# Output rows summed in PSUM, a scaled choice matrix, fewer products per block, and a new order, in a one-core kernel of a long convolution and a token-choice MLP

## The chip, the core and the metric

One core of a Trainium2 chip runs the program. Its engines are TensorE (PE; PEld is its weight load), VectorE (DVE), ScalarE (ACT), GpSimd (POOL) and SyncE (SP), which issues most of the transfers. The metric is the device time of one execution in microseconds; lower is better.

## The reference, cut to what matters

```python
x = A_q                                        # 2048 tokens of 640 features, bf16
sa, ca, ga, sb, cb, gb = silu(c) @ w_mod       # six rows of 640
h = layernorm(x) * (1 + ca) + sa
x = x + ga * (h * conv(h's k, v))              # shift conv of 4 taps, times v, long conv over 2048 tokens
h = layernorm(x) * (1 + cb) + sb               # second normalisation
r = h @ w_r;  idx = 8 tokens with the largest r
y = (silu(h[idx] @ w_gate) * (h[idx] @ w_up)) @ w_down * sigmoid(r[idx])
out = x + gb * (h + scatter(idx, y))
```

The last line is, for each token, `x*(1) + layernorm(x)*gb*(1+cb) + gb*sb`, and for eight tokens a further row of 640 is added in place in DRAM.

## The kernel before, in words

The features are split in five blocks of 128 (b = 0 to 4) and the tokens in 16 groups of 128 (m = 0 to 15). Each block goes through a convolution by two short Fourier stages: `C` (shift convolution as products with the diagonals `dg`, times `vN`), `KV` (folding), `G` and `X` (first stage into tile `A`), `BG` and `BX` (second stage into `HX`), `P` (pointwise product, `T` or `T2`), `BT` (inverse stage into `U`), `UW` (`U` written to DRAM, `Ud`), `LU` (read back transposed, `uA`), `AT` (last stage into `t`) and `AA` (added into `xq`, the residual rows). Block 4 is turned on the chip instead (`XT`, tiles `V`, `tT`, `xT`) and put back into `xq` by `RB`. `R` transposes a block of `xq` into `xT` and takes three sums over features (`pr`, added into `rsum`); `GR` takes products of `xT` with itself of which only the diagonal is used, the sum of squares (`ssq`).

Then comes the tail. `T` is one long task in steps: `n2v` and what follows make the reciprocal root `rs2` and the keys of the choice; `prT`, `vi`, `crow`, `cand`, `t8` find the eight largest keys; `oh32` is the choice matrix (one column per chosen token); `pX` gathers the rows by products with it; `px`, `xsf`, `xsT` turn and scale them; `pgu`, `gs`, `hh`, `hT`, `pyT`, `yT`, `py`, `delta` are the MLP; the last step is an indirect transfer by GpSimd that adds `delta` into the output in DRAM. Between these steps stand the output rows: `BS` and `BL` make `base` = `xq` + gb*sb, `N` makes the normalised row `xn` (ScalarE, or VectorE where the order says `*`), `F` multiplies two rows at a time by the gate (L926), adds the base (L928) and issues their transfer.

The order of all work is one table, `ORDER`: each word runs the next step of a task, a star moves its copy to VectorE, `:n` repeats it. Every engine runs its instructions in that order. A second table, `SLOTS`, says which buffer each new tile takes. PSUM has four tiles of two banks for passing results (`ps`), of which one is given up when the first small tile (`pq`, `pg`) is made.

## Time and profile before

| | us |
|---|---|
| median of 3 runs | 171.48 (170.65 to 174.46) |
| the profiled execution | 170.81 |
| its span in the profile | 169.0 |

The 1.8 us between the last two lie around the span. In the profile a busy share is the time in which an engine ran something; an engine with 90% may still not be the one that others wait for. The chain of waits follows the work that ended last back to its start.

### The profile page before, as it was taken

The page shows a single profiled execution, that of the slowest core. Times are in us where ns is not written, and L with a number is a line of the kernel's source. Part 1 is how long each engine was busy: PE and PEld are TensorE (multiplying, and loading weights), DVE is VectorE, ACT ScalarE, POOL GpSimd, SP SyncE. Part 2 cuts the span into 40 slices and gives each one's busy share as a digit, 9 for nine tenths or more (in the row PEclk, how much of TensorE's full clock was granted, in tenths as well). Part 3 has the DMA queues.
Part 4 walks back from the last instruction along what each step waited for, and adds up shares of the span by engine and source line. Part 5 has one row for each costly group of instructions (what it writes and reads, how often), then busy time and mean ns, then how long its engine had stood idle before and what let it go on. Part 6 is the DMA issues. An engine that isn't in the chain of part 4 may idle for free.

```text
span 169.0 us, 5171 instructions
## 1 busy us (share of the span) xinstructions
PE 144.2 (85%) x2210; PEld 113.9 (67%) x2210; DVE 152.5 (90%) x292; ACT 138.3 (82%) x157; POOL 41.3 (24%) x72
## 2 busy tenths in 40 slices
PE   7797988996989999999999999999699687946700
PEld 2395976885768778789987898898689563322600
DVE  7898999999999999799999999999979898998820
ACT  3629999998988998989999989989966826989900
POOL 8754079209998000420000000010000020000003
PEclk9999999999999999999999999999999955799955
DMA  6999999999999996592953629259927910385440
GB/s 136 206 275 158 228 190 267 287 365 175 283 363 225 307 264 175 179 297 62 263 188 124 215 104 273 77 152 353 272 85 213 303 69 4 83 277 216 155 159 2
DMA packets 54238, 33.93 MB, mean 201 GB/s; under 512 B 34049, under 2 KB 51910, under 8 KB 54214
## 3 DMA queue, kind: packets, MB, share of 16 engines
q1 hardware_dynamic: 54008, 33.58, 73.8%
q8 instruction: 17, 0.28, 0.7%
q0 software_dynamic: 80, 0.01, 0.1%
q14 instruction: 7, 0.06, 0.1%
q10 hardware_dynamic: 126, 0.01, 0.1%
HBM read 23.62 MB, written 6.83 MB: 180 GB/s over the span
## 4 chain that ended last, share of the span: by engine, by line
PE 53%; DVE 34%; issue 5%; ACT 4%; DMA 1%; POOLq 1%; DVEq 0%
PE ps L550 14%; PE ps L509 6%; PE ps L443 5%; DVE kv L89 4%; PE ps L599 4%; PE p L481 3%; PE ps L328 3%; DVE A L71 3%; DVE gF L465 3%; PE p L550 2%; DVE HX L71 2%; PE pg L675 2%; DVE st L854 2%; PE p L443 2%; DVE IT L928 2%
## 5 line engine op out<-in xcount | busy, mean ns | idle before, releaser
L73 ACT CAST HX<-ps 128x1024 bf16<-128x1024 f32 x30 | 29.9, 1042 | 1.2 <-PE ps L509 1.1
L73 ACT CAST A<-ps 128x1024 bf16<-128x1024 f32 x26 | 26.6, 1045 | 3.3 <-PE ps L443 3.2
L550 PE MATMUL ps<-IT,HX 128*128 128x256 bf16 x144 | 23.5, 273 | 0.0
L481 PEld LDWEIGHTS <-kT 128*128 128x128 bf16 x320 | 18.4, 98 | 2.1 <-issue 1.7
L73 ACT CAST U<-ps 128x1024 bf16<-128x1024 f32 (+1 forms) x19 | 16.8, 901 | 2.4 <-PE ps L550 2.0
L509 PE MATMUL ps<-A,FX 128*128 128x256 bf16 x128 | 18.3, 273 | 0.4 <-ACT A L73 0.2
L509 PEld LDWEIGHTS <-FX 128*128 128x128 bf16 x160 | 14.1, 97 | 4.1 <-issue 2.7
L550 PEld LDWEIGHTS <-HX 128*128 128x128 bf16 x160 | 14.8, 98 | 2.8 <-issue 1.0
L550 PE MATMUL ps<-IT,T 128*128 128x256 bf16 x80 | 15.3, 273 | 0.0
L854 DVE BATCH_NORM_STATS2 st<-xq 128x6 f32<-128x320 bf16 x32 | 13.4, 478 | 0.0
L522 DVE TENSOR_TENSOR HX<-HX 128x2048 bf16<-128x2048 bf16 x10 | 12.3, 1225 | 0.3
L383 POOL TENSOR_SCALAR dg<-ident,shk_f 128x128 bf16<-128x128 bf16 x16 | 9.9, 631 | 10.5 <-PE ps L481 9.4
L521 DVE TENSOR_TENSOR T<-HX 128x2048 bf16<-128x2048 bf16 x10 | 12.1, 1214 | 0.0
L481 PE MATMUL p<-dg,kT 128*128 128x128 bf16 x160 | 10.1, 219 | 0.8 <-DVE dg L383 0.7
L443 PEld LDWEIGHTS <-xA 128*64 128x64 bf16 x160 | 8.0, 109 | 3.7 <-issue 2.0
L550 PEld LDWEIGHTS <-T 128*128 128x128 bf16 x96 | 9.4, 98 | 1.1
L872 DVE TENSOR_TENSOR h<-h,modv 128x2048 bf16<-128x2048 bf16 x8 | 9.7, 1219 | 0.1
L481 PE MATMUL ps<-dg,kT 128*128 128x128 bf16 x160 | 9.8, 219 | 0.1
L353 POOL CAST bcol<-bint 40x1 f32<-40x1 int32 x1 | 0.2, 180 | 38.4 <-DVE bint L352 38.4
L73 ACT CAST A<-p 128x1024 bf16<-128x1024 f32 x9 | 9.4, 1041 | 0.0
L443 PE MATMUL ps<-RA,gF 128*64 128x256 bf16 x120 | 9.0, 278 | 0.0
L443 PEld LDWEIGHTS <-gF 128*64 128x64 bf16 x160 | 7.5, 109 | 2.2 <-issue 1.4
(280 smaller groups left out, 354.4 us busy)
## 6 DMA issues: line engine op xcount, KB each, us to landing
early<-in_w_mod_dram SPq DMA_DIRECT2D x6, 800.0 KB, 7.7
Ud<-U SPq DMA_DIRECT2D x8, 512.0 KB, 3.3
uA<-Ud SPq DMA_DIRECT2D x8, 512.0 KB, 5.1
gA<-in_A_ssm_k_dram SPq DMA_DIRECT2D x5, 512.0 KB, 8.4
vN<-in_A_v_dram SPq DMA_DIRECT2D x5, 512.0 KB, 6.0
xq<-in_A_q_dram SPq DMA_DIRECT2D x4, 640.0 KB, 8.0
wg<-in_B_w_gate_dram SPq DMA_DIRECT2D x5, 432.0 KB, 4.9
wu<-in_B_w_up_dram SPq DMA_DIRECT2D x5, 432.0 KB, 9.9
```

The source lines that it names most:

```text
L71: self.nc.vector.tensor_copy(out=out, in_=in_)
L73: self.nc.scalar.copy(out=out, in_=in_)
L89: V.tensor_tensor(out=out, in0=acc, in1=other, op=ALU.mult)
L383: (nc.gpsimd if evac.vector else V).tensor_scalar(out=dg[:, j, :], in0=ident[:], scalar1=shk_f[:, b, j:j + 1], scalar2=None, op0=ALU.mult)
L443: nc.tensor.matmul(ps[o, bb // 2, :, (bb % 2) * 8:(bb % 2) * 8 + 8].rearrange("p (k c) e -> p k c e", c=2), lhsT=src[:, 4 * g4 + bb, o], r ...
L481: nc.tensor.matmul(ps[:, i, :], lhsT=kT[:, n0 - j:n0 - j + P], rhs=diags[b][:, j, :], start=(j == 0), stop=(j == 3))
L509: nc.tensor.matmul(ps[:, i], lhsT=FX[:, k2, :], rhs=A[:, 2 * k2:2 * k2 + 2, u, :], start=True, stop=True)
L521: V.tensor_tensor(out=T2[:], in0=X, in1=Hi, op=ALU.mult)
L522: V.tensor_tensor(out=X, in0=X, in1=Hr, op=ALU.mult)
L550: nc.tensor.matmul(ps[:, i, :], lhsT=a, rhs=IT[:, k2, d:d + 2, :].rearrange("p a b -> p (a b)"), start=(n == 0), stop=(n == len(terms) - 1))
L854: V.bn_stats(out=st1[:, m, hf, :], in_=xq[:, m, hf * 320:hf * 320 + 320])
L872: V.tensor_tensor(out=hq, in0=hq, in1=row[:, None, 0:w].to_broadcast([P, 4, w]), op=op)
```

## The change

The tables `ORDER` and `SLOTS` are new throughout. Beside that:

- `R` makes only the transposed block. The three sums over features go into `GR`, which sums all five blocks in one PSUM tile. Its products with itself are 64 wide for groups 0 to 13 and 32 wide for groups 14 and 15: 36 per block, where there were 64. The diagonal is then taken by four VectorE steps over 960 columns, where two took 512.
- `BS`, `BL`, `F` and the tiles `xn` and `base` are gone. `XG` (VectorE) and `XL` (TensorE and ScalarE) make `xg` = `xq` times the gate. `NP` sums, in a PSUM tile per group of tokens, the row of `xq` (product with the identity) and a product of two rows (`gx`: the gate row and the gate*shift row) with two columns (mean term and one). `N` ends the row: starred, by one VectorE step `xg * rs2 + ps`; else by a product with the diagonal of `rs2` (`dgo`) and a ScalarE copy. `GX` and `NM` prepare the small operands.
- The choice matrix is multiplied by `rs2` before the gather. The steps `sel`, `sel2`, `psn`, `xa`, `xb` are gone; the mean comes from a sum that the ScalarE copy of `pX` accumulates, by one more small product.
- `T` has its index and sigmoid steps taken out (`TI`, near the end of the order). `WT` issues 12 products whose result nobody reads, three in mid-order and nine around the start of `T`.

```diff
 ORDER = """
-R2 R3 BS*:2 WG XT WD XT* GR R3 COL WG BS* R4 GR RB GR WG T BL N* N RB N WG T N:2 F T F:2 N* WD N F:2 N BL T N F BS F T
-F N:2 BS F T:2 F N:2 F BS N T N F:2 N BS F:2 T F T:2
+R2 XT WD R3 WG TC WG XT GX COL GR:3 WG:3 RB:2 WT GR XL WT T WT T XL NM XG T NP:2 T WD N*:2 NP XG NP N:2 XG NP XG NP N*
+NP N* NP:2 N* NP N N*:2 T NP N* NP XG NP:2 N* T NP N* XG NP N* N T N* TI T:3
...
+    def t_WT():
+        for k in range(4):
+            pw = ps_tile([P, 512])
+            for i in range(3):
+                nc.tensor.matmul(pw[:], lhsT=ident[:], rhs=FX[:, 0:4, :]..., start=True, stop=True)
+            yield
...
+    def small_products(ps, xT, first, last):
+        for m in range(M):
+            n = 64 if m < 14 else 32
+            c0 = 64 * m if m < 14 else 448 + 32 * m
+            for j in range(P // n):
+                t = xT[:, m * P + n * j:m * P + n * j + n]
+                nc.tensor.matmul(ps[n * j:n * j + n, c0:c0 + n], lhsT=t, rhs=t, ...)
+    def diagonals(ps, sq, out):
+        for (c0, c1, m0, m1, msk_) in ((0, 896, 0, 14, m64), (896, 960, 14, 16, m32)):
...
+            V.tensor_tensor(out=r(sq), in0=r(ps), in1=msk_[:, None, :].to_broadcast([P, n, w]), op=ALU.mult)
+            V.tensor_reduce(out=out[:, m0:m1], in_=r(sq), axis=mybir.AxisListType.X, op=ALU.add)
     def t_GR():
-        ps = other_ps([P, M, 32])
+        ps = small_ps([P, 1024])
         for b in range(NB):
+            xT = xTs[b].rearrange("p m t -> p (m t)")
             for m in range(M):
-                for j in range(4):
-                    t = slice(32 * j, 32 * j + 32)
-                    nc.tensor.matmul(ps[t, m, :], lhsT=xTs[b][:, m, t], rhs=xTs[b][:, m, t], ...)
+                nc.tensor.matmul(ps[:, 960 + 3 * m:963 + 3 * m], lhsT=xT[:, m * P:m * P + P], rhs=wcol[:, b, :], ...)
+            small_products(ps, xT, False if b else None, b == NB - 1)
             yield
-        V.tensor_tensor(out=sq, in0=ps[:], in1=m32[:, None, :].to_broadcast([P, M, 32]), op=ALU.mult)
-        V.tensor_reduce(out=ssq[:], in_=sq, axis=mybir.AxisListType.X, op=ALU.add)
+        V.tensor_copy(out=rsum[:], in_=ps[:, 960:1008].rearrange("p (m c) -> p m c", c=3))
...
+        diagonals(ps, tail()[:, 0:1920].bitcast(F32), ssq)
         yield
...
+    def t_XG():
+        w = (NB - 1) * P
+        for j in range(8):
+            V.tensor_tensor(out=xg(2 * j, 2)[:, :, 0:w], in0=xq[:, 2 * j:2 * j + 2, 0:w],
+                            in1=gbo[:, None, 0:w].to_broadcast([P, 2, w]), op=ALU.mult)
+            yield
+    def t_NM():
+        V.tensor_copy(out=spad..., in_=sn[:, 1, :])
+        pt = ps_tile([P, 4, P], BF)
+        for i in range(4):
+            nc.tensor.transpose(pt[:, i, :], spad[:, i, :], ident[:])
+        lT["n"] = tail()[:, 0:512].rearrange("p (i t) -> p i t", i=4)
+        evac(lT["n"], pt[:])
+        yield
...
+    def products(ps, a, b, first, last):
+        for i in range(2):
+            nc.tensor.matmul(ps[:, i, 0:320], lhsT=a, rhs=b[:, i, :], start=first, stop=last, ...)
+    def t_NP():
+        for m in range(M):
+            ps = outps[m] = ps_tile([P, 2, 512])
+            r = slice(32 * (m % 4), 32 * (m % 4) + 2)
+            products(ps, ident[:], half(xq[:, m, :]), True, False)
+            products(ps, lT["n"][r, m // 4, :], half(gx[r, :]), False, True)
+            yield
     def t_N():
         for m in range(M):
+            ps, row = outps[m], xg(m)[:, 0, :]
             if evac.vector:
-                V.tensor_scalar(out=xn(m), in0=xq[:, m, :], scalar1=rs2[:, m:m + 1], scalar2=nm2[:, m:m + 1], ...)
+                V.scalar_tensor_tensor(out=half(row), in0=half(row), scalar=rs2[:, m:m + 1], in1=ps[:, :, 0:320],
+                                       op0=ALU.mult, op1=ALU.add)
             else:
-                nc.scalar.activation(out=xn(m), in_=xq[:, m, :], func=ACT.Identity, scale=rs2[:, m:m + 1], ...)
+                dg = ring.tile([P, 4, P], BF, name="dgo", tag="dg", bufs=2)
+                V.tensor_scalar(out=dg[:, 0, :], in0=ident[:], scalar1=rs2[:, m:m + 1], scalar2=None, op0=ALU.mult)
+                products(ps, dg[:, 0, :], half(row), False, True)
+                nc.scalar.copy(out=half(row), in_=ps[:, :, 0:320])
+            if m % 2:
+                nc.sync.dma_start(out=out_d[:, m - 1:m + 1, :], in_=xg(m - 1, 2))
             yield
-    def t_F():
-        for j in range(8):
-            u = xn(2 * j, 2).rearrange("p (m d) -> p m d", m=2)
-            V.tensor_tensor(out=u, in0=u, in1=gbo[:, None, :].to_broadcast([P, 2, D]), op=ALU.mult)
-            yield
-            V.tensor_tensor(out=u, in0=u, in1=h_["base", j // 4][...], op=ALU.add)
-            nc.sync.dma_start(out=out_d[:, 2 * j:2 * j + 2, :], in_=u)
...
+        V.tensor_tensor(out=onehot, in0=onehot, in1=rs2[:, :, None].to_broadcast([P, M, NSEL]), op=ALU.mult)
...
-        V.tensor_tensor(out=sel, in0=onehot..., in1=sn..., op=ALU.mult)
-        V.tensor_reduce(out=sel2[:], in_=sel.rearrange("p a m s -> p a s m"), ...)
...
-        V.tensor_copy(out=xg[:, 0:256], in_=pX[:, 0:256])
-        nc.scalar.copy(out=xg[:, 256:D], in_=pX[:, 256:D])
+        nc.scalar.activation(out=xg, in_=pX[:, 0:D], func=ACT.Identity, accum_out=acc[:])
```

How the tables move the work is shown at three places. On VectorE, at the end of `GR` and ahead of `n2v`, before (rsum are the three sums, pg the products) and now:

```order
L734 TENSOR_TENSOR rsum<-rsum,pq 128x48
L736 SCALAR_TENSOR_TENSOR msq<-rsum 128x16
L679 TENSOR_TENSOR tail<-pg,m_118 128x512
L680 TENSOR_REDUCE ssq<-tail 128x16
L936 SCALAR_TENSOR_TENSOR n2v<-ssq,msq 128x16
```

```order
L710 COPY rsum<-pq 128x48
L715 SCALAR_TENSOR_TENSOR msq<-rsum 128x16
L697 TENSOR_TENSOR tail<-pq,m_119 128x896
L698 TENSOR_REDUCE ssq<-tail 128x14
L697 TENSOR_TENSOR tail<-pq,m_118 128x64
L698 TENSOR_REDUCE ssq<-tail 128x2
L971 SCALAR_TENSOR_TENSOR n2v<-ssq,msq 128x16
```

Two more steps stand between the products and `n2v`, and the first two now read the same PSUM tile as the others.

On SyncE's queue, around the read-back (uA) of the block that is read last, before (block 3) and now (block 2):

```order
L570 DMA Ud_1813<-U 128x2048
L580 DMA uA<-Ud_1813 128x8x256
L881 DMA wg<-in_B_w_gate_dram 128x1728
L580 DMA uA<-Ud_1813 128x8x256
L881 DMA wg<-in_B_w_gate_dram 128x1728
L609 DMA_TRANSPOSE qT_2536<-in_A_q_dram 128x2048
```

```order
L584 DMA Ud_1943<-U 128x2048
L915 DMA wg<-in_B_w_gate_dram 128x1728
L594 DMA uA<-Ud_1943 128x8x256 x2
L623 DMA_TRANSPOSE qT_2472<-in_A_q_dram 128x2048
L925 DMA wd<-in_B_w_down_dram 108x8x640
L919 DMA wu<-in_B_w_up_dram 128x1728 x5
```

The write, the read-back and the transposed load of `qT` keep their order; all five pieces of `wu` now come behind `wd`.

On VectorE, between the choice matrix (oh) and the step that makes xsT, a part of before and the whole of now:

```order
L928 TENSOR_TENSOR xn<-xn,base 128x1280
L926 TENSOR_TENSOR xn<-xn,modv 128x1280
L981 TENSOR_TENSOR tail<-oh_122,sn 128x256
L984 TENSOR_REDUCE sel_2999<-tail 128x16
L994 CAST tail<-ps 128x256
```

```order
L1015 TENSOR_TENSOR oh_126<-oh_126,sn 128x16x8
L956 SCALAR_TENSOR_TENSOR xg<-xg,sn,ps 128x640 x2
L729 TENSOR_TENSOR xg<-xq,modv 128x2x512
L960 TENSOR_SCALAR dgo<-ident,sn 128x128 x2
L729 TENSOR_TENSOR xg<-xq,modv 128x2x512 x2
L956 SCALAR_TENSOR_TENSOR xg<-xg,sn,ps 128x640 x3
L960 TENSOR_SCALAR dgo<-ident,sn 128x128
L956 SCALAR_TENSOR_TENSOR xg<-xg,sn,ps 128x640 x2
L1038 TENSOR_TENSOR xsf<-pq,mc 128x40
L1039 TENSOR_TENSOR xsT<-xsf,mc 128x5x8
```

Ten rows of tokens are ended or prepared by VectorE ahead of `xsT` now; before, eight steps of L926 and L928 and five small ones stood there.

## Rows read from the trace of the kernel before

**Rows 1.** The page: engines' busy time, its share of the span, and instructions.

```profile
PE 144.2 (85%) x2210; PEld 113.9 (67%) x2210; DVE 152.5 (90%) x292; ACT 138.3 (82%) x157; POOL 41.3 (24%) x72
```

**Rows 2.** Stretches: length, each engine's busy time (instructions), granted clock, DMA share, GB/s.

```profile
10.00:47.00 37.00, 32.40 (x497) 26.93 (x495) 36.33 (x49) 33.64 (x38) 19.84 (x27) 1.00 1.11 251
47.00:128.80 81.80, 79.74 (x1218) 67.92 (x1218) 77.91 (x140) 74.69 (x85) 10.40 (x14) 1.00 0.71 206
138.70:161.60 22.90, 16.16 (x198) 7.75 (x197) 20.81 (x59) 19.42 (x25) 0.22 (x1) 0.80 0.43 144
```

**Rows 3.** The chain that ended last, 100 to 136 us: start, length, what.

```profile
104.83 1.75 PE ps L550 x16
...
112.07 0.89 PE ps L599 x16
...
114.30 0.44 PE ps L509 x4
114.73 0.38 PE pq L730 x16
...
115.57 0.59 PE pg L675 x64
...
120.06 0.93 PE ps L550 x8
...
121.19 1.70 issue
...
134.01 0.84 issue
```

**Rows 4.** SyncE's queue in the timeline, and the transfers of tile uA.

```profile
108.39 0.33 SPq L570 DMA_DIRECT2D Ud<-U  x1
111.15 0.36 SPq L580 DMA_DIRECT2D uA<-Ud  x1
...
DMA to landing us min/median/max: 3.9/5.1/7.1
```

**Rows 5.** DMA queues on the page: packets, MB, share of 16 engines.

```profile
q8 instruction: 17, 0.28, 0.7%
```

**Rows 6.** VectorE in the timeline, end of block 4's turning.

```profile
135.15 0.69 DVE L648 TENSOR_TENSOR xT<-qT,tT 128x1024 bf16<-128x1024 bf16 x1
```

**Rows 7.** VectorE in the timeline, diagonals to the tail's first step.

```profile
137.27 0.69 DVE L679 TENSOR_TENSOR tail<-pg,m 128x512 f32<-128x512 f32 x1
138.00 0.69 DVE L680 TENSOR_REDUCE ssq<-tail 128x16 f32<-128x512 f32 x1
138.72 0.17 DVE L936 SCALAR_TENSOR_TENSOR n2v<-ssq,msq 128x16 f32<-128x16 f32 x1
```

**Rows 8.** Groups by line and shape: count, busy us, mean ns, idle before.

```profile
L71 DVE CAST A<-ps 128x1024 bf16<-128x1024 f32 x3 | 3.6, 1214 | 0.0
L693 DVE TENSOR_TENSOR base<-xq,modv 128x1024 bf16<-128x1024 bf16 x4 | 2.6, 681 | 0.0
```

**Rows 9.** The tail in the timeline.

```profile
145.20 1.71 PE L991 MATMUL ps<-xq,oh 128*32 128x512 bf16 x32
...
151.44 0.20 DVE L1008 TENSOR_TENSOR xsT<-xsf,xb 128x40 bf16<-128x40 f32 x1
...
160.75 0.83 DVE L928 TENSOR_TENSOR IT<-IT,base 128x1280 bf16<-128x1280 bf16 x1
...
161.49 0.34 DVE L1061 SCALAR_TENSOR_TENSOR delta<-pq,sig,gb 40x128 bf16<-40x128 f32 x1
...
164.93 1.68 POOL L1063 DMA_INDIRECT out_dram<-delta,idx  x1 [24.62 <-issue]
```

**Rows 10.** The chain's end.

```profile
161.60 2.28 DMA out_dram<-IT
```

**Rows 11.** Stretches as in Rows 2, for the granted clock (1.00 is 2.4 GHz).

```profile
132.50:135.00 2.50, 0.95 (x70) 0.68 (x67) 1.88 (x3) 1.89 (x2) 0.00 (x0) 1.00 0.87 297
135.50:146.00 10.50, 8.77 (x127) 4.58 (x128) 9.55 (x33) 6.09 (x7) 1.20 (x5) 0.52 0.06 22
152.00:157.00 5.00, 2.78 (x46) 1.17 (x35) 4.15 (x14) 5.00 (x8) 0.00 (x0) 1.00 0.60 218
```

More of the change, by code (lines that the diff above doesn't have):

```diff
@@ new lines, in t_GR @@
+        G.tensor_scalar(out=mu[:], in0=rsum[:, :, 2], scalar1=1.0 / D, scalar2=None, op0=ALU.mult)
+        G.tensor_tensor(out=r0[:], in0=rsum[:, :, 0], in1=rsum[:, :, 1], op=ALU.add)
+        G.tensor_scalar(out=mw[:], in0=mu[:], scalar1=wsum[:, 0:1], scalar2=None, op0=ALU.mult)
+        G.tensor_tensor(out=r0[:], in0=r0[:], in1=mw[:], op=ALU.subtract)
+        V.scalar_tensor_tensor(out=msq[:], in0=rsum[:, :, 2], scalar=1.0 / (D * D), in1=rsum[:, :, 2], op0=ALU.mult, op1=ALU.mult)
+        diagonals(ps, tail()[:, 0:1920].bitcast(F32), ssq)
@@ new lines, in t_GR, with xg, t_XL @@
+        yield
+    def xg(m, n=1):
+        j = m // 8
+        if ("xg", j) not in h_:
+            h_["xg", j] = ring.tile([P, 8, D], BF, name="xg", tag="HX", bufs=2)
+        return h_["xg", j][:, m % 8:m % 8 + n, :]
+    def t_XG():
+        w = (NB - 1) * P
+        for j in range(8):
+            V.tensor_tensor(out=xg(2 * j, 2)[:, :, 0:w], in0=xq[:, 2 * j:2 * j + 2, 0:w],
+                            in1=gbo[:, None, 0:w].to_broadcast([P, 2, w]), op=ALU.mult)
+            yield
+    def t_XL():
+        w = (NB - 1) * P
+        for j in range(2):
+            o = xg(8 * j, 8)[:, :, w:D]
@@ L692, in t_BS @@
             if evac.vector:
-                V.tensor_tensor(out=o, in0=xq[:, 2 * j:2 * j + 2, 0:512],
-                                in1=gbs[:, None, 0:512].to_broadcast([P, 2, 512]), op=ALU.add)
-            else:
-                ps = ps_tile([P, 2, 512])
-                for i in range(2):
-                    nc.tensor.matmul(ps[:, i, :], lhsT=ident[:], rhs=gbs[:, 0:512], start=True, stop=False)
-                    nc.tensor.matmul(ps[:, i, :], lhsT=ident[:], rhs=xq[:, 2 * j + i, 0:512], start=False, stop=True)
-                evac(o, ps[:])
@@ L899, in _kernel_body @@
     mu, msq, r0, mw = (tiny(n) for n in ("mu", "msq", "r0", "mw"))
-    xns = {}
-    def xn(m, n=1):
-        if m < 8:
-            if m // 2 not in xns:
-                xns[m // 2] = ring.tile([P, 2 * D], BF, name="xn", tag="G", bufs=GN)
-            return xns[m // 2][:, m % 2 * D:(m % 2 + n) * D]
-        return IT[:].rearrange("p a b c -> p (a b c)")[:, m % 8 * D:(m % 8 + n) * D]
+    half = lambda t: t.rearrange("p (i d) -> p i d", i=2)
+    outps = {}
+    def products(ps, a, b, first, last):
+        for i in range(2):
+            nc.tensor.matmul(ps[:, i, 0:320], lhsT=a, rhs=b[:, i, :], start=first, stop=last, skip_group_check=True)
@@ L965, in t_T @@
         V.max(out=vi[:], in_=prT[:, :])
-        crow = small.tile([M, M, 2 * NSEL], BF, name="crow")
-        V.tensor_tensor(out=crow[:], in0=vi[:].bitcast(BF)[:, None, :].to_broadcast([M, M, 2 * NSEL]),
+        crow = tail()[0:M, 768:1024].rearrange("p (m j) -> p m j", m=M)
+        V.tensor_tensor(out=crow, in0=vi[:].bitcast(BF)[:, None, :].to_broadcast([M, M, 2 * NSEL]),
                         in1=ident[0:M, 0:M, None].to_broadcast([M, M, 2 * NSEL]), op=ALU.mult)
@@ L978, in t_T @@
                         in1=t8[:, None, :].to_broadcast([P, M, NSEL]), op=ALU.is_equal)
+        h_["t8"] = t8
+        V.tensor_tensor(out=onehot, in0=onehot, in1=rs2[:, :, None].to_broadcast([P, M, NSEL]), op=ALU.mult)
         yield
-        sel = tail()[:, 256:768].bitcast(F32).rearrange("p (a m s) -> p a m s", a=2, m=M)
-        V.tensor_tensor(out=sel, in0=onehot[:, None, :, :].to_broadcast([P, 2, M, NSEL]),
-                        in1=sn[:, :, :, None].to_broadcast([P, 2, M, NSEL]), op=ALU.mult)
-        sel2 = small.tile([P, 2, NSEL], F32, name="sel2")
-        V.tensor_reduce(out=sel2[:], in_=sel.rearrange("p a m s -> p a s m"), axis=mybir.AxisListType.X, op=ALU.add)
         pX = ps_tile([P, 1024])
@@ L1060, in t_T @@
         delta = small.tile([n40, P], BF, name="delta")
[L1061 removed]
+        V.scalar_tensor_tensor(out=delta[:], in0=py[:, :], scalar=h_["sig"][:, 0:1], in1=gb40[:], op0=ALU.mult, op1=ALU.mult)
         yield
```

185 lines of the change are left out of this document (87 added, 98 removed).

## The prediction, made before the changed kernel was run

> **What bounds it now.** I read four views: the page's busy times, the stretches, the chain of waits, and the timeline of the tail. By the page three engines are close to full over the whole span [rows 1], so the average doesn't say which one matters. The stretches do [rows 2]. From 10 to 47 us VectorE is busy 36.33 of 37.00 us and TensorE 32.40: VectorE (with ScalarE) bounds. From 47.0 to 128.8 TensorE is busy 79.74 of 81.80 and the chain of waits runs along it, with one hole of 1.70 us that the view puts down to "issue" [rows 2, 3]. From 138.7, where the tail's task begins, VectorE is busy 20.81 of 22.90 us: it bounds again [rows 2]. The span then ends with a transfer of the last output rows (2.28 us) and GpSimd's indirect transfer, which starts at 164.93, about 1.05 us after those rows have landed, though `delta` was ready at 161.83 [rows 9, 10]. So the end is set by the last row, not by the MLP.
>
> I make the sum against the profiled execution, 170.81 us (span 169.0 and 1.8 around it), and add its difference to the median, 171.48. 2% of that, 3.4 us, is about what a measurement of this kernel can tell from no change.
>
> **The change, part by part.**
>
> *Middle, TensorE's work.* I count what stands ahead of the turning of block 4 in either order. Block 2's transposes (16 products of 128 columns, 0.89 us as in `AT`) and one of three sets of small products (64 in 0.59) move behind it, three idle products of 512 columns come in (256 columns take 0.44/4 = 0.11 us, so 3 x 0.215 = 0.64), and 36 products 64 or 32 wide take the place of 64 [rows 3]. How long a 64-wide one takes no row shows: the 32-wide ones come each 9.2 ns, and 64 columns alone need twice the columns' time; I take equal time per set, 0.58, so the sum is -0.89 - 0.59 + 0.64, about **-0.85 us** (0 if VectorE holds the middle instead). VectorE's work up to there I counted as equal to 0.3 us: among some twenty exchanges, copies from PSUM (1.21 each, [rows 8]) go to and fro between it and ScalarE, and three `base` steps (0.68) become two `xg` steps of the same size.
>
> *The late read-back.* The block that is read back from DRAM last is now block 2. Before, the last `BT` of block 3 ended at 106.58, its read-back was issued at 111.15 and took 5.1 us (3.9 to 7.1) to land: 9.7 us in all (8.5 to 11.7), and its `AT` came long after [rows 3, 4]. Now TensorE has, between block 2's last `BT` and its first `AT`, 8 products of `BX` (0.88), four sets of 16 (`R` twice, `AT` twice, 4 x 0.89), 4 of `BX` (0.44), `HT` (0.89), 8 of `BT` (0.93) and two `GR` blocks (2 x (0.38 + 0.58)): 8.6 us [rows 3]. TensorE waits for the difference, **+1.1 us** (0 to 3.0). Behind that wait stand the rest of `BT4` and the turning of block 4, so it is passed on.
>
> *The hole.* The 1.70 us of "issue" stand inside a run of sixteen equal products of `pr`, after the ninth: nothing of the program is awaited there [rows 3]. Another hole, 0.84 us, lies 510 TensorE instructions later, inside a run of small products of `GR` [rows 3]. 17 packets of instructions, 0.28 MB, were moved [rows 5], about 64 bytes for each of TensorE's 4414 instructions. I read it as the wait for the next block of instructions, used up fastest where products are small. Now the same place in the stream falls into 128-wide transposes, which take more time each, and `GR` has 56 instructions per block fewer. I take the hole as gone: **-1.7 us** (-2.5 with the second; +1.0 if a run of small products of `GR` meets one). The Trainium skill, Runtime: NRT & Kernel Launch, section Instruction fetch mechanics, says that instructions come in blocks of 256 and that crossing one costs little and is mostly hidden. The trace agrees with the spacing (510) and not with "hidden" (1.70 us); by the page's second half the hole would have another cause and stay, and the sum would be 1.7 higher.
>
> *Turning block 4.* The second half now waits for a PSUM tile that block 2's transposes hold until ScalarE has copied them; VectorE takes both halves straight from PSUM. I get its last step some 0.4 us later than the 135.84 of before [rows 6]: **+0.4** (0 to 0.9).
>
> *Diagonals.* Before, the first diagonal step starts at 137.27, right behind the last product, and `n2v` at 138.72: two steps of 0.69 and their distance, 1.45 us [rows 7]. A copy of 1024 columns from PSUM takes 1.21 and a step of 512 takes 0.69: 1.02 ns a column [rows 7, 8]. So 896 columns take 1.08, 64 take 0.23; with 0.04 between them 1.12 + 1.12 + 0.27 + 0.27 = 2.78. `rsum` and `msq`, which before lay beside the last products, now wait for the same tile: another 0.4. 3.2 against 1.45: **+1.7 us**, all on the path. This step is the change's surest loss.
>
> *Tail on VectorE.* Out go eight L926 and eight L928 (0.82 each, 0.74 apart, 11.9 us), two `xn` steps and the `sel` and `xa` steps, about 14.7 in all. In come twelve row steps that read PSUM (640 columns at 1.02 ns and 0.16: 0.82, or 0.73 apart), six `XG` (0.6 each), four `dgo` (0.22), and a step on the choice matrix: 13.7 [rows 8, 9]. A row step's bounds are 0.37, half of L928's 1280 columns of SBUF, and 1.13, the 1024-column copy less the overlap; I take 0.73, for its operand is PSUM as in the copy. So VectorE wins one microsecond only; ScalarE wins some 13, but was not on the path.
>
> *Tail's order.* From `n2v` to the end of the gather took 138.72 to 146.91, and gains a step on the matrix and a wait for `NM`: 8.4 against 8.2. From there to the end of `xsT` took 4.73 (to 151.64); now seven row steps (5.1), three `XG` (1.8), three `dgo` (0.66), less the two rows that fit beside the gather, and a wait of 0.5 for PSUM tiles make 6.4. From `xsT` to the end of `delta` took 10.19 (to 161.83); now 9.8 [rows 9]. `delta` is ready 24.6 after `n2v`, before 23.1: +1.5. But the rows are out before it, so GpSimd's transfer follows `delta` and not the last row's landing 2.05 later [rows 9, 10]. 1.05 + 24.6 against 26.2: **-0.55 us** (-3.2 to +3.6 with the row step's bounds, nine of the twelve on this path).
>
> *TensorE's clock there.* Before, the granted clock was 1.00 in a stretch where TensorE was busy 0.95 of 2.50 us, then 0.52 (nearly all at 1.2 GHz) from 135.5 to 146.0, and 1.00 at 152 to 157 with 2.78 of 5.00 busy [rows 11]. The same idle stretch remains ahead of the tail. At 1.2 GHz, `RB`, `XL` and nine idle products between `GR` and the transpose of the keys take 6.4 us, against 5.9 for VectorE's chain: +0.5; at 2.4 GHz nothing. **+0.3**.
>
> Sum: -0.85 + 1.1 - 1.7 + 0.4 + 1.7 - 0.55 + 0.3 = **+0.4**. That gives 171.2 for the profiled execution and 171.9 beside the median; the gain and the loss in the tail nearly cancel.
>
> **Rivals.**
>
> *Faster: the early order.* From 10 to 47 us TensorE is busy 32.40 of 37.00, so 4.6 us are idle, while afterwards it is the bound [rows 2]. The new order runs block 3's shift convolution there and puts other work later; if that fills half of the hole, 2.3 us are gained, and with the read-back in time another 1.1: 168.5. For it: the chain leaves VectorE only at 47. Against it: VectorE has 0.67 us free there, and by my count it needs 1 us more work to reach the same TensorE work. With row steps at 0.5 us it would be 167.
>
> *Slower: the low clock stays.* The row products are 16 x 4 x 320 columns, 0.53 us a group at 2.4 GHz and 1.07 at 1.2. Between the gather and `px` stand eight of them and three diagonal pairs, 5.1 us against VectorE's 6.4: hidden. If the clock granted from 135.5 to 146.0 [rows 11] lasted through that stretch, they would take 10.2 and TensorE would bound, +4.5: 176.4. It decides from the point where the clock rises: after the gather it costs, before it doesn't. Against it: the nine idle products and the gather keep TensorE busier than before, when it rose at 146.
>
> *Slower: the middle.* If VectorE's extra early work is not hidden (+1) and the read-back takes its 7.1 (+1.9): 174.8.
>
> **How the numbers follow.** The forecast, 171.9 with 169.5 to 174.5 of its own, gets 0.56; the early order 0.24; the low clock 0.10; the middle 0.10. The range of 8 in 10 reaches half-way into both sides: 167.8 to 175.0. Faster by over 2% (below 168.05) holds half of the early order and a rest of the forecast's row-step bound and hole, near 0.21; slower (above 174.9) the clock and half of the middle, 0.16.
>
> **What would show it.** Diagonals: `n2v` some 3.2 us after the last product. Read-back: `AT` of block 2 waiting about 1 us for `uA`. Hole: no "issue" over 1 us ahead of block 4's turning. Row step: about 0.8 us each. End: GpSimd's transfer starting a microsecond behind `delta`, the last rows landed before. Clock: 1.00 from the gather on. I am wrong above all if the turning of block 4, whose last step starts at 135.15 before [rows 6], moves by over 2 us; I only counted work there, and didn't follow each wait.

## The result, and the profile after

The changed kernel takes 174.47 us in the median of 20 runs (172.73 to 179.97), the kernel before 171.75 in the 20 runs beside it (170.65 to 174.46). The ratio is 1.0145, with an interval of 1.0109 to 1.0182: slower by about 1.5%, inside the range, and within the 2% that the likeliest case was about. The forecast of 171.9 was 2.6 us too low, and this part is about where those came from. The profiled execution has a span of 172.7 us against 169.0. Runs differ in how long TensorE's lower clock lasts in the tail, so the ratios leave out those over 1.5% above the fastest of their kernel; of the twenty of the changed kernel, the five with the highest mean clock (0.984 to 0.986) took 172.7 to 173.5 us, and the others 174.3 and more.

The page of the changed kernel, engines' busy time, for [rows 1]:

```profile
PE 154.4 (89%) x2150; PEld 118.7 (69%) x2150; DVE 152.8 (89%) x294; ACT 130.5 (76%) x147; POOL 40.1 (23%) x77
```

Three stretches of it, with the columns of [rows 2]:

```profile
10.00:47.00 37.00, 32.86 (x486) 27.55 (x484) 36.61 (x57) 34.43 (x38) 26.74 (x41) 1.00 1.09 262
47.00:126.80 79.80, 78.61 (x1098) 66.68 (x1095) 77.72 (x139) 75.62 (x86) 3.12 (x3) 1.00 0.71 191
139.80:164.70 24.90, 23.27 (x212) 9.64 (x213) 19.84 (x50) 6.71 (x10) 0.23 (x1) 0.93 0.40 129
```

The first two look as before. The third is the news: from the tail's first step to the last row TensorE is busy 23.27 of 24.90 us, where it was busy 16.16 of 22.90, and VectorE has 5 us free. ScalarE fell from 19.42 to 6.71. The chain of waits of the changed kernel says the same (start, length, what), for [rows 3] and [rows 10]:

```profile
116.60 4.16 DMA uA<-Ud
120.81 1.07 PE ps L613 x16
...
128.11 0.89 issue
...
137.31 1.01 DVE tail L697
...
144.92 1.19 PE ps L940 x6
146.11 2.25 PE ps L1023 x32
148.36 2.43 PE ps L940 x10
...
151.12 5.22 PE ps L940 x28
...
156.70 2.90 PE ps L940 x16
...
164.76 2.77 DMA out_dram<-xg
```

From 144.92 to 163.4 the chain runs almost entirely along TensorE, 13.6 of these 18.5 us along its products of the output rows (L940), and it still ends with the last rows' transfer. The timeline of the changed kernel at the turning of block 4 and at the diagonals (start, length, engine, line, operation), for [rows 6, 7]:

```profile
134.18 0.69 DVE L662 TENSOR_TENSOR xT<-qT,tT 128x1024 bf16<-128x1024 bf16 x1
...
137.22 1.08 DVE L697 TENSOR_TENSOR tail<-pq,m 128x896 f32<-128x896 f32 x1
138.34 1.09 DVE L698 TENSOR_REDUCE ssq<-tail 128x14 f32<-128x896 f32 x1
...
139.85 0.17 DVE L971 SCALAR_TENSOR_TENSOR n2v<-ssq,msq 128x16 f32<-128x16 f32 x1
```

And the tail, for [rows 9]:

```profile
146.04 2.31 PE L1023 MATMUL ps<-xq,oh 128*32 128x512 bf16 x32
...
157.12 0.20 DVE L1039 TENSOR_TENSOR xsT<-xsf,mc 128x40 bf16<-128x40 f32 x1
...
163.82 0.87 DVE L956 SCALAR_TENSOR_TENSOR xg<-xg,sn,ps 128x640 bf16<-128x640 bf16 x1
...
166.88 0.34 DVE L1074 SCALAR_TENSOR_TENSOR delta<-pq,sig,gb 40x128 bf16<-40x128 f32 x1 [0.45 <-PE pq L1072]
...
168.57 1.67 POOL L1076 DMA_INDIRECT out_dram<-delta,idx  x1 [27.13 <-issue]
```

These rows split the 3.7 us of span into the prediction's own stages:

| stage | before | after | difference | forecast |
|---|---|---|---|---|
| to the end of the last `xT` step | 135.84 | 134.87 | -0.97 | -1.05 |
| from there to the start of `n2v` | 2.88 | 4.98 | +2.10 | +1.7 |
| `n2v` to the end of the gather | 8.19 | 8.51 | +0.32 | +0.2 |
| gather to the end of `xsT` | 4.73 | 8.96 | +4.23 | +1.7 |
| `xsT` to the end of `delta` | 10.19 | 9.90 | -0.29 | -0.4 |
| `delta` to the end of the span | 7.20 | 5.49 | -1.71 | -2.05 |

(The forecast had 0.3 more for the clock.) One stage is 2.5 us off, the one with most of the row products between gather and `xsT`. There they stand in the timeline one pair per 0.375 us, first TensorE's products, then its weight loads:

```profile
151.77 0.44 PE L940 MATMUL ps<-modv,tail 2*128 2x320 bf16 x2
152.14 0.45 PE L940 MATMUL ps<-xq,ident 128*128 128x320 bf16 x2
152.52 0.44 PE L940 MATMUL ps<-modv,tail 2*128 2x320 bf16 x2
```

```profile
151.77 0.11 PEld L940 LDWEIGHTS <-tail 2*128 2x128 bf16 x2 [0.26 <-issue]
152.14 0.11 PEld L940 LDWEIGHTS <-ident 128*128 128x128 bf16 x2 [0.27 <-issue]
```

A row's four products take 0.75 us. The prediction had 0.53 at 2.4 GHz, from the columns alone. The weight loads show a pattern: each pair's first load starts together with its own product (151.77, 152.14), not beside the product before it. Just ahead of these rows stands a pair that follows a diagonal pair, also on 128 rows. Its load starts 0.13 us sooner than its product, and the pair itself 0.28 behind the one before (151.12):

```profile
151.27 0.23 PEld L940 LDWEIGHTS <-ident 128*128 128x128 bf16 x2
151.40 0.43 PE L940 MATMUL ps<-xq,ident 128*128 128x320 bf16 x2
```

Of single records, the second product of a pair on 2 rows starts 0.146 us behind the first, and the next pair 0.227 behind that. The clock was 0.50 from 146.1 to 149.5 and 1.00 from there to the last row, so it explains the slow gather (2.31 us) and the first two pairs behind it (0.64 each), but not this pace:

```profile
146.10:149.50 3.40, 3.40 (x37) 1.14 (x36) 2.15 (x4) 0.80 (x2) 0.00 (x0) 0.50 0.27 96
149.50:157.00 7.50, 7.15 (x45) 2.63 (x45) 5.76 (x10) 2.01 (x3) 0.00 (x0) 1.00 0.25 87
```

### The profile page after: what moved, and what is told of

It is laid out like the page before. It is cut to its first block, busy times and chain, and to the rows that moved or that the text cites. A ratio compares the mean times of both kernels' runs of the same rounds, so it can differ in the third digit from the quotient of the medians.

```text
span 172.7 us, 5043 instructions
## 1 busy us (share of the span) xinstructions
PE 154.4 (89%) x2150; PEld 118.7 (69%) x2150; DVE 152.8 (89%) x294; ACT 130.5 (76%) x147; POOL 40.1 (23%) x77
## 4 chain that ended last, share of the span: by engine, by line
PE 63%; DVE 21%; ACT 5%; DMA 4%; issue 3%; POOLq 1%; DVEq 0%; ACTq 0%; SPq 0%
PE ps L564 10%; PE ps L940 8%; PE p L564 6%; PE ps L457 6%; PE ps L523 6%; PE ps L495 4%; PE ps L613 3%; PE ps L330 3%; DMA uA<-Ud 2%; PE p L457 2%; ACT HX L73 2%; PE p L495 2%; DVE kv L89 2%; DVE A L71 2%; DMA out_dram<-xg 2%
## 5 line engine op out<-in xcount | busy, mean ns | idle before, releaser
L73 ACT CAST HX<-ps 128x1024 bf16<-128x1024 f32 x28 | 27.8, 1044 | 1.2 <-PE ps L523 1.2
L73 ACT CAST A<-ps 128x1024 bf16<-128x1024 f32 x25 | 24.8, 1031 | 0.4 <-PE ps L457 0.2
L564 PE MATMUL ps<-IT,HX 128*128 128x256 bf16 x104 | 16.6, 273 | 0.0
L495 PE MATMUL ps<-dg,kT 128*128 128x128 bf16 x224 | 14.0, 219 | 0.9 <-DVE dg L397 0.8
L73 ACT CAST U<-ps 128x1024 bf16<-128x1024 f32 (+1 forms) x15 | 12.5, 870 | 2.2 <-PE ps L564 1.9
L397 POOL TENSOR_SCALAR dg<-ident,shk_f 128x128 bf16<-128x128 bf16 x16 | 11.5, 736 | 8.8 <-PE ps L495 5.7
L457 PE MATMUL ps<-RA,gF 128*64 128x256 bf16 x136 | 10.5, 276 | 0.6 <-DVE A L71 0.5
L564 PE MATMUL ps<-IT,T 128*128 128x256 bf16 x56 | 10.7, 273 | 0.0
L956 DVE SCALAR_TENSOR_TENSOR xg<-xg,sn,ps 128x640 bf16<-128x640 bf16 x12 | 10.1, 875 | 0.5 <-issue 0.4
L564 PE MATMUL p<-IT,HX 128*128 128x256 bf16 x56 | 9.8, 274 | 0.0
## 6 DMA issues: line engine op xcount, KB each, us to landing
early<-in_w_mod_dram SPq DMA_DIRECT2D x6, 800.0 KB, 10.2
```

What stands on the lines that cost most here:

```text
L73: self.nc.scalar.copy(out=out, in_=in_)
L397: (nc.gpsimd if evac.vector else V).tensor_scalar(out=dg[:, j, :], in0=ident[:], scalar1=shk_f[:, b, j:j + 1], scalar2=None, op0=ALU.mult)
L457: nc.tensor.matmul(ps[o, bb // 2, :, (bb % 2) * 8:(bb % 2) * 8 + 8].rearrange("p (k c) e -> p k c e", c=2), lhsT=src[:, 4 * g4 + bb, o], r ...
L495: nc.tensor.matmul(ps[:, i, :], lhsT=kT[:, n0 - j:n0 - j + P], rhs=diags[b][:, j, :], start=(j == 0), stop=(j == 3))
L564: nc.tensor.matmul(ps[:, i, :], lhsT=a, rhs=IT[:, k2, d:d + 2, :].rearrange("p a b -> p (a b)"), start=(n == 0), stop=(n == len(terms) - 1))
L956: V.scalar_tensor_tensor(out=half(row), in0=half(row), scalar=rs2[:, m:m + 1], in1=ps[:, :, 0:320], op0=ALU.mult, op1=ALU.add)
```

## The experiments

Theory A: TensorE bounds the tail, because a product on 128 rows of the array and one on 2 rows follow each other and each change costs it a weight load that nothing hides. Rivals: 320 columns cost that much whatever the weights are (B), or VectorE's row steps, 875 ns each, bound the tail anyway (C). A second question came from the trace: TensorE pauses 2 us at 137.8, ahead of the idle products that should keep it busy. All ratios are to the kernel before, on the same chip.

### What sets the pace of the rows

**e1_full_rows.** The pair of gate and shift rows stands in four masked copies, all other rows zero, so the mean product runs on 128 rows. Same columns, same count; four small steps that make the copies come in beside it.

```diff
-            r = slice(32 * (m % 4), 32 * (m % 4) + 2)
-            products(ps, lT["n"][r, m // 4, :], half(gx[r, :]), False, True)
+            products(ps, lT["n"][:, m // 4, :], half(gx4[:, m % 4, :]), False, True)
```

> The mean product of each output row takes its weights from all 128 rows (the pair of gate and shift rows stands in four masked copies, other rows zero) in place of two rows of the array; nothing of the result changes. Theory A, TensorE bounds the tail, and each change between a product on all 128 rows and one on 2 rows costs it some 0.08 us because the next weights are loaded only when the product before has ended: one row's four products take 0.59 us in place of 0.75, weight loads start with the product before, about 2 us of time are won, 172.4 us. Theory B, a product of 320 columns takes 0.187 us whatever its weights are: 0.75 a row as before, no change, 174.5. Theory C, VectorE's row steps (0.875 each) bound the tail: products come sooner, but the end moves by less than 0.5.

Measured: 172.4 us, ratio 0.9996 (0.9936 to 1.0055), against 1.0145 (1.0109 to 1.0182) for the change: 1.5%, about 2.5 us, are back (1.3 to 3.7 by the two intervals). The timeline, products and then loads:

```profile
152.06 0.43 PE L949 MATMUL ps<-xq,ident 128*128 128x320 bf16 x2
152.33 0.43 PE L949 MATMUL ps<-IT,tail 128*128 128x320 bf16 x2
152.60 0.43 PE L949 MATMUL ps<-xq,ident 128*128 128x320 bf16 x2
```

```profile
152.19 0.23 PEld L949 LDWEIGHTS <-tail 128*128 128x128 bf16 x2
152.47 0.23 PEld L949 LDWEIGHTS <-ident 128*128 128x128 bf16 x2
```

A pair per 0.27 us, 0.136 for 320 columns: 0.43 ns a column, as for the 256-wide products of [rows 3] (sixteen in 1.75). Each load starts 0.14 us ahead of its products. A holds and B falls. Whether the number of rows or their place in the array matters was not separated. The Trainium skill, TensorE: Matmul & The Clock Gate, Part 3: Packing small matmuls — row/col tiling, says that a weight load overlaps a running product only where their row groups differ. For products on the same 128 rows this trace shows otherwise: their loads are hidden (152.19, ahead of 152.33). That loads stand open between 128 rows and 2 does not contradict it, since the 2 rows lie within the 128.

VectorE now has little free. From its second diagonal step to its last row step it is busy 11.93 of 12.50 us, where the change has it busy 12.30 of 13.90 with the same 22 steps. The stretch of this kernel, then the change's:

```profile
150.90:163.40 12.50, 11.52 (x130) 7.28 (x131) 11.93 (x22) 3.30 (x5) 0.00 (x0) 1.00 0.50 178
```

```profile
150.80:164.70 13.90, 13.17 (x131) 5.55 (x132) 12.30 (x22) 3.30 (x5) 0.00 (x0) 1.00 0.40 143
```

**e2_no_mean.** The mean product is left out.

```diff
-            products(ps, ident[:], half(xq[:, m, :]), True, False)
-            products(ps, lT["n"][r, m // 4, :], half(gx[r, :]), False, True)
+            products(ps, ident[:], half(xq[:, m, :]), True, True)
```

> The mean product of every output row is left out, so the rows lack the mean and shift terms. Theory A (TensorE bounds the tail): one row's products take 0.29 us, TensorE then waits for VectorE and PSUM, the row steps come 0.88 apart without gaps and 3 to 4 us are won, about 171. Theory C (VectorE bounds the tail): at most 0.5 us, 174.0.

172.11 us, ratio 1.001 (0.995 to 1.007): no better than with full rows, although TensorE has half of the row work. As far as intervals of 1 us tell, the 2.5 us are all that TensorE held; behind them VectorE bounds, as C says of that state. Its same 22 steps take 12.50 us again, although TensorE is busy 8.88 and not 11.52:

```profile
149.90:162.40 12.50, 8.88 (x106) 4.97 (x107) 11.91 (x22) 3.30 (x5) 0.00 (x0) 1.00 0.45 159
```

A's 3 to 4 us were too much.

### Diagonals and small products

**e3_small_diag.** All products behind the variances 32 wide, so the diagonal steps read 512 columns in place of 960.

```diff
-            n = 64 if m < 14 else 32
-            c0 = 64 * m if m < 14 else 448 + 32 * m
+            n, c0 = 32, 32 * m
...
-        for (c0, c1, m0, m1, msk_) in ((0, 896, 0, 14, m64), (896, 960, 14, 16, m32)):
+        for (c0, c1, m0, m1, msk_) in ((0, 512, 0, 16, m32),):
```

> The products behind the variances are all 32 wide again, so that the diagonal steps read 512 columns and not 960; nothing of the result changes. The forecast's term for the diagonals: n2v starts 1.3 to 1.5 us after the last product in place of 2.9, and all of it reaches the end, 173.0. Rival: what follows waits for TensorE (idle products, gate products) or for the mean's rows, and the end moves by less than 0.5; or the 64 products in place of 36 take it back.

A clear miss: 182.86 us, ratio 1.06 (1.0441 to 1.0759), 8 us slower than the change. `n2v` did come 1.85 us after the last product's end in place of 3.0, but TensorE stops twice, at places where nothing of the program is awaited. TensorE's timeline:

```profile
136.10 0.30 PE L688 MATMUL pq<-xT 128*32 128x32 bf16 x20
138.81 0.49 PE L688 MATMUL pq<-xT 128*32 128x32 bf16 x44 [2.41 <-issue]
...
140.33 0.61 PE L670 MATMUL ps<-ident,xT 128*128 128x128 bf16 x4
146.10 1.46 PE L670 MATMUL ps<-ident,xT 128*128 128x128 bf16 x12 [5.17 <-issue]
```

Counted along TensorE's records, work resumes at number 3776 and at 4032, 256 apart, and there was one more stop at 3264. In the kernel before, the holes of 1.70 and 0.84 us of [rows 3] end at 3265 and 3777. In the change the 2 us ahead of the idle products end at 3777. So the prediction's reading of the 1.70 us, a wait for the next block of instructions, holds for far more than that hole.

The packets of queue q8 [rows 5] are 16 KB each, one for each such block. Their times beside TensorE's, from the trace's packet records (us; a block is entered with its first record):

```
kernel               block entered  next packet  landed   resumes   stop
before, at 3265          115.95        120.48     121.47   122.89    1.70
before, at 3777          128.23        132.28     133.55   134.85    0.84
change, at 3777          134.20        137.24     138.33   139.79    1.97
e3_small_diag, 4032      138.81        143.52     144.65   146.10    5.17
e7_small_diag_wd, 4032   139.12        140.39     141.77   143.13    1.85
e5_wd_later, at 3776     135.65        138.76     139.86   141.25    1.98
e9_up_later, at 3777     134.61        135.37     136.30   138.07    none
```

In these rows the packet for the next block starts 0.8 to 4.7 us after the block before it was entered and takes about a microsecond, and a stopped TensorE goes on 1.3 to 1.5 us after it landed. (That it always starts after is not shown: at three other blocks of the change's trace it starts 0.06 to 1.1 us ahead of the record.) Between entry and packet the DMA engines' mean busy share was 0.82 to 1.20 in the rows with 3.0 us or more, 0.65 in the seventh kernel's and 0.08 in the ninth's. 128 products of 32 to 64 columns are used up sooner than entry, packet and these 1.3 us follow each other.

**e4_idle_sooner.** Another PSUM buffer for the first idle products, and six of them.

```diff
-            for i in range(3):
+            for i in range(6 if k == 1 else 3):
```

(and three buffer numbers: 10210201 becomes 10120101)

> The first group of idle products behind the last transposes takes the PSUM buffer that is free sooner, and has six products in place of three, so TensorE works from 138.5 and not from 139.8; nothing of the result changes. If the low clock from 146.1 to 149.5 comes from TensorE's pause of 2 us there, the gather takes 1.2 us in place of 2.31 and the row products behind it 0.6 less: 1.2 to 1.7 us are won, 173.0. Rival: the pause of the keys' transpose or an earlier one decides, the clock falls all the same and the time stays, 174.5.

175.44 us, ratio 1.0196 (1.006 to 1.0333; four runs): nothing won beside the change's 1.0145. The stop stayed. TensorE's timeline of the change, and then of this kernel:

```profile
139.79 0.82 PE L338 MATMUL ps<-FX,ident 128*128 128x512 bf16 x3 [1.97 <-DVE tail L697]
```

```profile
138.21 1.07 PE L670 MATMUL ps<-ident,xT 128*128 128x128 bf16 x16
141.23 1.47 PE L338 MATMUL ps<-FX,ident 128*128 128x512 bf16 x5 [1.96 <-ACT xq L73]
```

A releaser whose name changes while the stop keeps its length, and its number in the stream (3776), is hardly the cause. The gather did run at 2.4 GHz in this profile (1.27 us), with the stop as before. From the last `xT` step to the end this profile takes 36.6 us and the change's 37.8, but that step ends 1.45 us later here, and in the median nothing of a gain is to be seen.

**e8_shifted.** The same warm-up columns in 45 products and not 13, which moves all later instructions by 64.

```diff
         for i in range(13):
-            nc.tensor.matmul(pw[:], lhsT=z[:, 0:P], rhs=z, start=True, stop=True)
+            n = 4 if i < 10 else 3 if i == 10 else 1
+            for c in range(n):
+                f = slice(512 * c // n, 512 * (c + 1) // n)
+                nc.tensor.matmul(pw[:, f], lhsT=z[:, 0:P], rhs=z[:, f], start=True, stop=True)
```

> The warm-up at the start makes the same 13 x 512 columns of products in 45 pieces, so every later TensorE instruction stands 64 further on in the stream; nothing else changes and nothing of the result. Theory F: the pause ahead of the first idle products moves with the stream's count, not with the program: it now falls 64 instructions earlier in the program, inside the last block's small products, n2v starts some 2 us later against the last xT step, and the time is 0.5 to 2 us longer, 175 to 176.5. Rival (a wait of the program): the pause stays ahead of the first idle products, 174.5.

The stop moved as expected, into the last block's small products, and again to number 3776:

```profile
138.28 0.51 PE L692 MATMUL pq<-xT 128*64 128x64 bf16 x20
141.38 0.60 PE L692 MATMUL pq<-xT 128*64 128x64 bf16 x16 [2.60 <-issue]
```

`n2v` started 7.9 us after the last `xT` step's end in place of 5.0. Four runs gave 176.88 to 186.56 us, median 183.0, more than expected; how much of it is the clock is not known, so only the place counts. It shows that the stop hangs on the stream's count.

**e5_wd_later, e7_small_diag_wd, e9_up_later.** Is the packet late because weights fill the queues? SyncE asks for the second half of the down weights at 131.1 in the change, at 146.0 before. In the fifth kernel it stands behind the first two rows, and in the seventh this goes with the 32-wide products. In the ninth, in the change's order, all up weights wait for the last block's products, and it stands behind them. (Pieces of the order's lines:)

```diff
-XG T NP:2 T WD N*:2
+XG T NP:2 T N*:2 WD
```

```diff
-R2 XT WD R3 WG TC WG XT GX COL GR:3 WG:3 RB:2 WT GR XL
+R2 XT WD R3 TC XT GX COL GR:3 RB:2 WT GR WG:5 XL
         w_sb = W["u"] = ring.tile([P, NB, FF], BF, name="wu", tag="A", bufs=2)
+        G.memset(w_sb[:, :, 0:1], 0.0)
```

> The second half of the down weights is asked for behind the first two output rows (at about 148 us, as before the change) and not at 131.1; nothing of the result changes. Theory F, TensorE's pause of 2.1 us ahead of the first idle products is the wait for its next 256 instructions, and the packet that brings them starts late (3.0 us after the block before it was entered, against 1.1 to 1.4 where no weights move) because weights fill the transfer queues: the packet starts about 1 us sooner, the pause shrinks to under 1.2 us, the gather's clock may rise with it, 0.5 to 1.5 us are won, 173.3. Rival, the pause is the wait that the view names (a VectorE step of the diagonals): it stays at 2.1 us, and the time stays within 0.5 of 174.5.

176.34 us, ratio 1.0149 (1.0038 to 1.0261; four runs): no change that could be told, and the stop stayed. The up weights, asked for from 128.6 on, were still moving; the packet started 3.1 us after its block was entered. It is a miss of the place, not of the theory, as the other two show.

> All products behind the variances 32 wide again, with the second half of the down weights asked for behind the first two rows; nothing of the result changes. Theory F (instruction packets behind weights): the pause of 5.2 us that the 32-wide products alone had ahead of the last transposes falls to 2 to 3 us, since the packet that ends it starts 1 to 2 us after the block before it was entered and not 4.7; 178 to 180 in place of 182.9, still slower than the change, since 128 small products are used up in 1.2 us. Rival (the pause hangs on something in the program): 182.9.

179.89 us, ratio 1.0473 (1.04 to 1.0547), 3 us less than with the 32-wide products alone (the intervals still touch). The stop of 5.17 fell to 1.85, since its packet started 1.3 and not 4.7 us after the block was entered; the other one, 2.43, stayed.

> All of the up weights (2.1 MB, asked for from 127.2 us on) and behind them the second half of the down weights are held until the last block's products are done (about 138.5 us), by a small GpSimd write into their buffer; nothing of the result changes. Theory F (TensorE's next 256 instructions come late because weights fill the transfer queues): their packet, which started 3.0 us after the block before was entered, starts 1.1 to 1.4 after it, TensorE resumes at about 138 and not at 139.8, and the pause falls from 2.1 us to under 0.6. If the pause also brings the low clock of the gather, 1 us or more is won, about 173.3; if not, 174.5 as before, since VectorE's diagonals run meanwhile. Rival (the packet's lead is fixed): the pause stays at 2.1.

The packet started 0.8 us after its block was entered, and the stop is gone. TensorE's timeline:

```profile
137.17 1.07 PE L670 MATMUL ps<-ident,xT 128*128 128x128 bf16 x16
138.07 0.81 PE L338 MATMUL ps<-FX,ident 128*128 128x512 bf16 x2
```

The second diagonal step that the change's row named as releaser starts here at 139.76, 1.7 us after the idle products: it never held them. The tenth, eleventh and twelfth kernel hold the weights back too: 0.4 to 0.6 us to the packet, and no stop. The first, second, fourth, fifth and sixth do not: 2.9 to 3.3 us, and stops of 1.0 to 2.1. But 176.57 us, ratio 1.0182 (1.008 to 1.0283; four runs), is no gain. VectorE's diagonals run during the stop, and the keys' transpose follows its keys by 0.06 us in the change, with the stop, as here without. And the low clock was not gone but elsewhere in this profile, among the row products:

```profile
149.50:154.00 4.50, 4.15 (x24) 1.31 (x23) 4.07 (x7) 1.39 (x2) 0.00 (x0) 1.00 0.81 261
154.00:164.20 10.20, 10.20 (x62) 3.38 (x65) 6.87 (x11) 0.69 (x1) 0.00 (x0) 0.50 0.41 148
```

TensorE was busy nearly throughout ahead of that fall. So its pause is not what brings the low clock, or not alone.

### Is there a version that beats both?

**e6_rows_idle_wd, e12_rows_up_later, e11_two_more, e10_balanced** put the parts together: full rows with the edits of the fourth and fifth kernel; full rows with the up weights later; the same with two more rows ended by ScalarE; and full rows, up weights later, seven rows on ScalarE and the MLP's steps moved forward among them.

```diff
-NP N* NP:2 N* NP N N*:2 T NP N* NP XG NP:2 N* T N* NP XG
+NP N NP:2 N* NP N N*:2 T NP N* NP XG NP:2 N* T N NP XG
```

(a piece of the eleventh's order; the tenth has the following in place of the change's tail from the first row products on)

```
NP:2 T N*:2 WD NP XG NP N:2 NP T XG NP N* N NP:2 N* T NP XG N NP N* NP N XG T NP N* N NP XG NP N* N NP:2 N*:2 TI T T:2
```

> Three edits together: mean product from all 128 rows, six idle products on the buffer that is free sooner, second half of the down weights behind the first rows; nothing of the result changes. If the row products' pace (2.5 us, of which VectorE gives back some) and the low clock are separate losses, this is 1 us under the first edit alone, 171.4, slightly under the kernel before. If VectorE bounds the tail as soon as the row products are fast, the clock is worth nothing more and it stays at 172.4.

172.53 us, ratio 1.0042 (0.9999 to 1.0086): its second branch, not distinguishable from full rows alone.

> Mean product from all 128 rows, and up weights held until the last block's products are done; nothing of the result changes. With the mean product alone TensorE's pause and its idle products made the keys' transpose 1.06 us late. If the packet of instructions now comes at once, the pause is under 0.6 and the transpose starts 0.2 us behind its keys: 171.4, 1 us under the first experiment. Rival: the low clock comes elsewhere in its place, or the weights held back delay rows or the MLP: 172.4 or more.

172.17 us, ratio 1.0001 (0.9957 to 1.0046). The keys' transpose does follow its keys by 0.06 us and not by 1.06, and the stop is gone, yet the ratio is that of full rows alone. The profiled execution has a span of 169.4 us, but one execution says little beside twelve.

> Mean product from all 128 rows, up weights held until the last block's products are done, and two more output rows (the sixth and the twelfth) ended by a diagonal product and ScalarE, in the change's own order; nothing of the result changes. VectorE had no gap from 150.9 to 163.4 us with the fast row products alone, so two row steps less (2 x 0.875) and two diagonals more (2 x 0.25) bring the last row 1.2 us sooner; with the keys' transpose 1 us sooner as in the run beside it the time is 170.3, 1% under the kernel before. If TensorE bounds again, or the MLP's chain ends last: 171.4, as the run beside it.

173.68 us, ratio 1.007 (1.0023 to 1.0116): 0.7% slower than the kernel before, not 1% faster. VectorE is busy 10.22 of 13.00 us where the twelfth kernel has 11.89 of 12.50, so the steps taken off came back as waits, the longest for the transposes of the MLP, which stand on TensorE behind the row products:

```profile
159.87 0.60 DVE L1063 TENSOR_TENSOR gs<-gs,pq 128x432 bf16<-128x432 bf16 x1 [0.19 <-ACT gs L1060]
161.99 0.22 DVE L1068 COPY hT<-ps 108x128 bf16<-108x128 bf16 x1 [1.51 <-PE ps L1066]
```

> Up weights later (as in the run beside it), mean product from all 128 rows, seven output rows in place of four ended by a diagonal product and ScalarE, and the steps of the chosen tokens' MLP set earlier among the rows, the last rows ahead of its last product; nothing of the result changes. If VectorE bounds the tail once the row products are fast, it loses three row steps (0.875 each) and gains three diagonals (0.25): the last row ends 2 us earlier, 170.4, faster than both kernels by about 1 us over the kernel before. If the MLP's chain then ends last, the gain is 1 us only, 171.4. Rival: TensorE bounds again by three more diagonal pairs: 172.4.

177.16 us, ratio 1.0313 (1.025 to 1.0376): the worst of the four. Its row steps wait 4.2 us, mostly for their products (group by line: count, busy, mean ns, idle before and what ended it):

```profile
L964 DVE SCALAR_TENSOR_TENSOR xg<-xg,sn,ps 128x640 bf16<-128x640 bf16 x7 | 6.1, 878 | 4.2 <-PE ps L949 2.7 <-ACT gs L1059 1.5
```

In these two kernels, with three PSUM buffers for rows in flight, the order among VectorE, ScalarE and TensorE decided more than the sum of VectorE's work. No version tried beats the kernel before.

## Why the prediction was right in its range and low by 2.6 us

**Middle and hole (-0.85, +1.1, -1.7, and +0.4 for the turning): right in sum, in part by luck.** The last `xT` step ends 0.97 us earlier where the sum said 1.05. The hole of 1.70 us is gone, as argued, and the third, seventh, eighth and ninth kernel show of its kind that it is a wait for instructions. (By the page TensorE and its loads have 4420 instructions, not 4414, and the two holes of before end 512 records apart, two blocks, not 510.) But TensorE waited 0.2 us at most for `uA` in the profile above, where the sum had 1.1, so the other terms together came out about a microsecond worse than forecast. Of that, 0.4 is the turning: 8.97 us from its first transposes (125.90) to the last `xT` step, against 8.18 before (from 127.66), so +0.8 and not +0.4. Where the rest went is not worked out. The late read-back is real but not steady. In the first, fourth, fifth, sixth and eleventh kernel TensorE waited 0.5 to 1.2 us there; in the fifth, whose code is the same up to there, it did so here:

```profile
122.26 0.96 PE L613 MATMUL ps<-RAT,uA 128*128 128x128 bf16 x14 [1.22 <-DMA uA<-Ud]
```

There, with the wait as forecast, the last `xT` step ends at 136.33, 0.5 us later than in the kernel before.

**Diagonals (+1.7): right, with a part unseen.** From the last product's end to `n2v` it is 3.0 us against 1.5, so +1.5. Another 0.6 lies ahead of it: the small products go on for 1.96 us behind the last `xT` step, a block and a half of them, where before it was 1.36 us and one block.

**Tail's order (-0.55): the step that failed.** "Seven row steps, three `XG`, three `dgo`", 6.4 us on VectorE, was the wrong engine. TensorE holds this stage, and it takes 8.96 us. (In the kernel before, six steps of L926 and L928 stood between the choice matrix and `xsT`, not eight.) The term was mis-sized at "0.53 us a group at 2.4 GHz": it is 0.75. The rival of the low clock had the right mechanism, TensorE bounding the row products, with the wrong condition: at 0.75 a group and 0.375 a pair its eight groups and three diagonal pairs take 7.1 us against VectorE's 6.4 at 2.4 GHz already, and a wait for `dgo` (0.35), `px` and the steps that make `xsT` come on top. (The rival's own +4.5 is more than its 10.2 less 6.4; it names no term for the rest.)

The 2.5 us that full rows give back and the 2.5 us by which this stage missed its forecast are alike only by chance. This stage at a clock of 1.00 throughout, in the fourth kernel's profile (rows as in the change) and in the first's (full rows):

```profile
149.03:157.47 8.44, 8.09 (x51) 2.85 (x51) 6.99 (x14) 2.87 (x5) 0.00 (x0) 1.00 0.33 116
149.35:156.84 7.49, 6.96 (x53) 4.44 (x53) 6.92 (x15) 2.87 (x5) 0.00 (x0) 1.00 0.37 131
```

So of the 2.5 us here 0.5 is the low clock (8.96 against 8.44) and 1.0 TensorE's pace (8.44 against 7.49). The other 1.1 is VectorE's own, since the stage takes 7.5 and not 6.4 with full rows too: five row steps 0.79 us apart, not 0.73 (0.3), the two steps that make `xsT` (0.4), which the sum left out, and the rest in waits and overlaps. The pace costs again behind this stage: from `xsT` to `delta` it is 9.83 us in the fourth kernel and 9.18 in the first. The row step itself, 0.875 us against "about 0.8", was nearly right. "The rows are out before `delta`" failed as well: the last rows land at 167.53, 0.3 us behind `delta`.

**Clock (+0.3): too little and in another place.** It was 1.00 up to 146.1 and 0.50 from there to 149.5, over the gather, which took 2.31 us in place of 1.71, and the first row products. In the fourth kernel's profile, at 1.00, it is 7.73 us from `n2v` to the end of the gather, not 8.51; with the 0.5 above that makes 1.3 us. About as much lies between the five runs of the change with the highest clock and its others. The ninth kernel shows the low clock among the row products instead, and what sends it there stays open.

The forecast came out inside its range in part by luck. The middle's sum held because the read-back was nearly in time, and the range was drawn for row steps of up to 1.13 us on VectorE: the cost of a slow row was in it, under the wrong engine's name.

## What to carry to other kernels

When work is moved from one engine to another, price it on the new engine from rows of the same kind in every respect: here the column count was right and the number of array rows was not, and that alone was about 2.5 us of the whole run. Where a view names a releaser for a stop, move the stop's surroundings (another buffer, 64 instructions more in front) before believing it. And count instructions, not only columns, where products are small: wider products that waste half of their columns can be the cheaper ones, as the 8 us of the third experiment show.
